# Next keys' products and counts in columns that scores leave empty, turned logits later, GpSimd's subtraction in two

## The chip, the cores and the metric

One core of one Trainium2 chip. The metric is the device time of one execution in microseconds (us), the median of three runs. The engines are named as in the profile: PE is TensorE's matmuls, PEld its weight loads, DVE VectorE, ACT ScalarE, POOL GpSimd, SP the engine whose queue issues most DMAs.

## The reference, cut to what matters

Attention over keys that are averaged from 4 x 4 blocks, and behind it a mixture of experts with one expert for each token. Four batches of 12288 tokens with 128 channels, 768 keys a batch, 8 experts with 1024 hidden units.

```python
kv_pool = kv.reshape(B, H // r, r, W // r, r, C).mean(axis=(2, 4))
k = v = kv_pool.reshape(B, -1, C) @ w_sr
s = q @ k.transpose(0, 2, 1) / np.sqrt(C)
a = np.exp(s - s.max(-1, keepdims=True))
a /= a.sum(-1, keepdims=True) + 1e-09
x = (a @ v).reshape(B * S, D)
logits = x @ w_gate
e_idx = np.argmax(logits, axis=1)
gate_w = softmax(logits)[np.arange(N), e_idx]
eom = 1.0 / (1.0 + np.exp(-(x @ w_output_gate)))
for e in range(E):
    h = np.maximum(x[mask] @ w1[e], 0.0)
    out[mask] = gate_w * eom[:, e] * (h @ w2[e])
```

## The kernel before, in words

The 49152 tokens are worked on in 96 groups of 512 (`NG`; 24 groups a batch, `GPB`). Nearly every product is split in fp16 halves, high and low, and made of three matmuls. For each batch one expert is chosen from the mean key, and all tokens go through it; tokens that want another expert are put on lists in DRAM and done at the end.

The order of work is written out by hand. The main loop runs over iterations `i` (one group enters in each) and eight steps `s`; `now[0]` is `8 * i + s`. In a step, the letters of `ORD` "shxryfue" say in which order things are issued: `s` the scores of 128 tokens (`qk`, on even steps, j = s // 2), `h` a hidden block of the expert for the group two iterations back (`moe_h`: H, HH on ScalarE, HL on VectorE), `x` the exponential (`qk_exp`), `r` the rounding of the probabilities (`qk_round`, on odd steps), `y` the expert's second product (`moe_y`), `f` a stage of the routing at step 5, `u` the product of probabilities and values (`pv`, which makes U and its two halves), `e` what `at(n, f)` has put down for this step. Behind the letters come, at the end of the step, the loads of queries, the next batch's keys (`kp`, the generator `kv_prep`), the transposes of probabilities (`p_turn`, a DMA on SP's queue), the splitting of weights (`w_split`) and the routing (`routes`). Each engine runs its instructions in the order in which they are issued.

PSUM has three pools: `psA` with two buffers of two banks (the scores S and whatever takes a tile "A"), `psH` with three of one bank (H, U, the logits, the turned logits), `psY` with one. A score uses columns 0 to 383 of each bank. Columns 384 to 511 hold the output's transposes (`moe_turn`, L822, for j of 2 and 3) and, through `hooks`, other small products: a hook is a function that is called with the S tile of the first score of j 0 or 1 (`HJ`; any j while i is 7 or less) from a given step on, ahead of its score's matmuls (L475 to L478), one for each S.

A score's way: PE makes S (L483 to L487), VectorE its maximum (L489, L490), ScalarE the exponential `pr` (L504, two buffers) and its fp16 rounding `ph` (L517), GpSimd the low half, `pr - ph`, as one operation of 128 x 768 (L518), SP's queue transposes both halves into PT (L523), and PE multiplies with the values (L540).

The next batch's keys (`kv_prep` with `fast` false, batches 1 to 3): for each of six blocks GpSimd adds rows (L296 to L300), five steps later PE transposes the sums into a psA tile kvt (L304), ScalarE copies them (L307), two steps later PE multiplies with w_sr into another psA tile kvk (L239), ScalarE copies the keys out (L240). Then the largest key is transposed in a psA tile vmp (L330) and read by `largest` (L170, L171), the fp16 halves K2 are made, V2 is transposed by DMA (L372), the expert is chosen through a hook (L376, L250), its weights are loaded (L717 to L722) and split by `w_split` (L770 to L778).

The routing runs once for a unit of four groups: `logits` (L550), `logits_turn` (L576) one step later (`RG`), then the generator `routing` (L594), a stage at a time: L611 to L617, L620 to L626, L628 to L637, then a hook with `counts` (L642, L643) for the next step on, L656 to L661, L663, the wait for the counts, their copy `cnt` out of S (L667), and so on to the list's rows, sixteen indirect DMAs on GpSimd's queue (L705).

Of the kernel before, what the change touches and what calls it, by code (L numbers as in the profile page):

```python
# [20 lines left out]
F32 = mybir.dt.float32  # L21
# [11 lines left out]
P = 128  # L33
# [21 lines left out]
class Cfg:  # L55
# [13 lines left out]
    SK, SO = 30, 15  # L69
    RG = 1  # L70
    RSEQ = (1, 2, 1, 1)
# [9 lines left out]
          (16, 0, (1, 1, 0)), (18, 0, (2, 1, 0), (1, 1, 1)), (20, 0, (2, 1, 1)))  # L81
    PRB = 2
    QL, QT, QN = 0, 3, 6
    QLA = ((7,), (7,)) + ((0, 3, 6),) * 6
# [16 lines left out]
def body(ctx, tc, q, kv, w_sr, w_gate, w_og, w1, w2, out, cfg=Cfg):  # L101
# [66 lines left out]
    def largest(m, ps):  # L168

        dve.tensor_reduce(out=m, in_=ps, op=ALU.max, axis=AX.X)  # L170
        dve.scalar_tensor_tensor(m, m, 2.0 ** -100, m, op0=ALU.max, op1=ALU.max)  # L171

# [58 lines left out]
    def kv_prep(b, fast):  # L231
# [4 lines left out]
        def keys(k, ps, pT):  # L236

            kk = ts(k, P)
            pe.matmul(ps[:, 1, 0:P], wsr, pT, start=True, stop=True)  # L239
            act.activation(kT[:, kk], ps[:, 1, 0:P], AF.Copy, accum_out=vs[:, k:k + 1])  # L240
# [33 lines left out]
        for k in range(NKB):  # L274
# [25 lines left out]
            pool.tensor_tensor(y[:, 1, 0:128], x[:, 1, 0:128], x[:, 1, 128:256], op=ALU.add)  # L300
            for _ in range(5):
                yield
            ps = psA.tile([P, 2, 512], F32, tag="A", name=f"kvt{b}_{k}")
            pe.transpose(ps[:, 0, 0:P], y[:, 1, 0:128], ident)  # L304
            KVN[b][1] += 1
            pT = kvp.tile([P, P], F32, tag="pT", name=f"pT{b}_{k}")
            act.activation(pT, ps[:, 0, 0:P], AF.Copy, scale=1.0 / 16.0)  # L307
            yield
            yield
            keys(k, psA.tile([P, 2, 512], F32, tag="A", name=f"kvk{b}_{k}"), pT)  # L310
            yield
        e2 = kvp.tile([P, 7], F32, tag="ve2", name=f"ve2{b}")
# [13 lines left out]
        if not fast:  # L326
            for _ in range(3):
                yield
        ps = psA.tile([P, 2, 512], F32, tag="A", name=f"vmp{b}")
        pe.transpose(ps[:, 0, 0:P], mxb, ident)  # L330
        if fast:
# [3 lines left out]
            warm(cfg.WM[1])  # L335
        largest(e2[:, 5:6], ps[:, 0, 0:P])
        powers(e2[:, 0:1], e2[:, 1:2], e2[:, 5:6])
# [122 lines left out]

    hooks, now, mid = [], [0], [False]
    spare = {"n": 0}

# [46 lines left out]
    def qk_round(i, j):  # L510

        pr = PR.pop((i, j))
        ph = wk.tile([P, 2, NK], F16, tag="ph", bufs=3, name=f"ph{i}_{j}")
        if j in cfg.PHD and i < LAG:
            dve.tensor_copy(ph[:, 0, :], pr)
        else:
            act.activation(ph[:, 0, :], pr, AF.Copy)  # L517
        pool.tensor_tensor(ph[:, 1, :], pr, ph[:, 0, :], op=ALU.subtract)  # L518
        PH[(i, j)] = (ph, None, now[0])
# [64 lines left out]

    WF = {}
    SCT = set()

# [6 lines left out]
    def routing(c):  # L594
# [11 lines left out]
        def T3(nm, n=E, bufs=1):  # L606
            return T(nm, n, F32, bufs).rearrange("p (b e) -> p b e", e=n)
# [33 lines left out]
        def counts(S):  # L641
            pe.matmul(S[:, 0, 384:384 + E], ones16, oh16, start=True, stop=True)  # L642
            pe.matmul(S[:, 1, 384:384 + E], tri16, oh16, start=True, stop=True)  # L643
            ps.append(S)

        ending = g0 + ng + 2 >= NG
        cnt = rt.tile([P, 2, E], F32, tag="cnt", name=f"cnt{c}")
        if ending:
            for _ in range(cfg.LC[c == NU - 1]):
                yield  # L650
            counts(psA.tile([P, 2, 512], F32, tag="A", name=f"cps{c}"))
            dve.tensor_copy(cnt, ps[0][:, :, 384:384 + E])
        else:
            hooks.append((now[0] + 1, counts))
        se = T("se")
        dve.tensor_reduce(out=se, in_=dn, op=ALU.add, axis=AX.X)  # L656
        zz = T3("dn")
        dve.tensor_tensor(zz, L[:, :, E:2 * E], oh, op=ALU.mult)
# [5 lines left out]
        while not ps:  # L664
            yield
        if not ending:
            dve.tensor_copy(cnt, ps[0][:, :, 384:384 + E])  # L667
        yield
# [13 lines left out]
        yield  # L682
        st = rt.tile([P, E], F32, tag="st", name=f"st{c}")
        dve.scalar_tensor_tensor(st, cnt[:, 1, :], -1.0, ebase, op0=ALU.add, op1=ALU.add)
        x1 = T3("x1")
# [7 lines left out]

        nd = rt.tile([P, E], F32, tag="nd", name=f"nd{c}")
        dve.scalar_tensor_tensor(nd, w8, cho, cnt[:, 0, :], op0=ALU.not_equal, op1=ALU.mult)
        dve.tensor_tensor(ebase, ebase, nd, op=ALU.add)
        rw = T3("rw", RW, 3)
        pool.tensor_copy(rw[:, :, 0:1], scl.unsqueeze(2))
# [287 lines left out]
    with tc.manual_schedule(engines={pool.engine, sp.engine, pe.engine, act.engine, dve.engine}):  # L986
# [32 lines left out]

        events = {}  # L1020

        def at(n, f, *args):
            events.setdefault(8 * i + s + n, []).append((f, *args))

        def after_values(ri, rc):
            if rc is not None:
                logits(rc)

                def turn():
                    logits_turn(rc)  # L1030
                    rts.append([routing(rc), 0, rc])
                at(cfg.RG, turn)
            n = max(0, 8 * cfg.UD + cfg.UDS * ri - now[0])
            at(cfg.UT + n, u_turn, ri)
            at(cfg.UO + n, u_out, ri)
# [190 lines left out]
```

## Time and profile before

| | us |
|---|---|
| median of 3 runs | 1962.98 (1962.57 to 1963.02) |
| the profiled execution | 1944.66 |
| its span, first to last instruction | 1942.9 |
| PE busy | 1870.8 (96%) |
| DVE busy | 1504.7 (77%) |
| ACT busy | 1321.3 (68%) |
| POOL busy | 1159.8 (60%) |

The profile is of one execution. Busy times are sums over the span; a matmul's end is modelled, and matmuls overlap in their pipeline. An idle time in brackets or in a list of waits is the time in which the engine ran nothing, with the instruction that ended it.

### The profile page before, as it was taken

What the parts mean: (1) busy time and instruction counts of PE and PEld (TensorE: products, weight loads), DVE (VectorE), ACT (ScalarE), POOL (GpSimd) and SP (SyncE); (2) the same over time, 40 slices, a digit from 0 to 9 for tenths busy, and PEclk for the clock granted to TensorE, in tenths of its full rate; (3) what the DMA queues carried; (4) which work ended last, traced back from release to release, by engine and by line L of the source; (5) the groups of instructions that cost most, each with busy time, mean ns of one, the idle gap of its engine ahead of it and who ended that gap; (6) DMA issues with size and microseconds to landing.
All of it is one profiled execution on the core that took longest, in us unless ns stands there. A gap on an engine that the chain in (4) does not pass through costs nothing. (4 is left out here: it accounts for less than half of the span.)

```text
span 1942.9 us, 31028 instructions
## 1 busy us (share of the span) xinstructions
PE 1870.8 (96%) x10225; PEld 951.0 (49%) x10225; DVE 1504.7 (77%) x3005; ACT 1321.3 (68%) x2391; POOL 1159.8 (60%) x996
## 2 busy tenths in 40 slices
PE   6999999999999999999999999999999999999997
PEld 4444455454445544545444554444445555545544
DVE  6776877888878778788787787787877877877773
ACT  3767767676776766676767776667677767767653
POOL 2537566564675676754756656656466456466462
PEclk9999999999999999999999999999999999999999
DMA  8877788788988887878788988778778778786642
GB/s 234 161 153 160 168 163 180 153 163 169 183 170 165 170 178 159 168 145 187 141 168 172 187 174 169 162 155 151 167 148 167 152 147 166 154 159 142 133 105 70
DMA packets 884017, 311.63 MB, mean 160 GB/s; under 512 B 827584, under 2 KB 833857, under 8 KB 883856
## 3 DMA queue, kind: packets, MB, share of 16 engines
q1 hardware_dynamic: 870944, 309.18, 78.7%
q0 software_dynamic: 12480, 0.40, 0.5%
q8 instruction: 81, 1.33, 0.3%
q14 instruction: 80, 0.66, 0.1%
q10 hardware_dynamic: 432, 0.07, 0.0%
HBM read 56.83 MB, written 51.25 MB: 56 GB/s over the span
## 5 line engine op out<-in xcount | busy, mean ns | idle before, releaser
L518 POOL TENSOR_TENSOR ph<-pr,ph 128x768 f16<-128x768 f32 x384 | 633.0, 1649 | 629.5 <-ACT ph L517 383.2
L796 DVE SCALAR_TENSOR_TENSOR HL<-H,HH 128x512 f16<-128x512 f32 x768 | 526.0, 686 | 142.3 <-ACT HH L795 127.9
L795 ACT ACTIVATE HH<-H 128x512 f16<-128x512 f32 x768 | 456.5, 594 | 246.6 <-PE H L792 240.3
L504 ACT ACTIVATE pr<-S,nm,qm 128x768 f32<-128x768 f32 x384 | 381.0, 992 | 240.2 <-DVE nm L490 222.7
L705 POOL DMA_INDIRECT scr<-rw,idx x384 | 383.1, 998 | 95.8 <-issue 88.1
L489 DVE TENSOR_REDUCE nm<-S 128x1 f32<-128x768 f32 x384 | 365.3, 951 | 86.8 <-PE S L487 86.3
L540 PE MATMUL U<-PT,V 128*128 128x512 f16 (+1 forms) x1746 | 406.1, 378 | 7.4 <-DVE HL L796 5.1
L517 ACT ACTIVATE ph<-pr 128x768 f16<-128x768 f32 x380 | 319.9, 842 | 2.4 <-DMA PT<-ph 1.9
L790 PE MATMUL H<-U,w 128*128 128x512 f16 x768 | 292.3, 381 | 12.3 <-DVE HL L796 7.0
L791 PE MATMUL H<-U,w 128*128 128x512 f16 x768 | 292.1, 380 | 0.0
L807 PE MATMUL Y<-HL,w 128*128 128x512 f16 x768 | 291.3, 379 | 0.7 <-DVE HL L796 0.6
L792 PE MATMUL H<-U,w 128*128 128x512 f16 x768 | 291.7, 380 | 0.0
L805 PE MATMUL Y<-HH,w 128*128 128x512 f16 x768 | 291.4, 379 | 0.3 <-ACT ys L810 0.3
L806 PE MATMUL Y<-HH,w 128*128 128x512 f16 x768 | 291.3, 379 | 0.0
L540 PEld LDWEIGHTS <-V 128*128 128x128 f16 x1746 | 171.4, 98 | 212.6 <-issue 11.5
L483 PE MATMUL S<-K,qT 128*128 128x384 f16 x768 | 189.2, 328 | 13.1 <-ACT pr L504 7.5
L487 PE MATMUL S<-K,qT 128*128 128x384 f16 x768 | 189.0, 328 | 1.3 <-DVE qT L459 1.0
L485 PE MATMUL S<-K,qT 128*128 128x384 f16 x768 | 188.9, 328 | 0.5 <-DVE K L349 0.5
L825 DVE TENSOR_TENSOR o<-S,msw 128x256 f32<-128x256 f32 x176 | 74.8, 425 | 89.0 <-ACT pr L504 87.6
L792 PEld LDWEIGHTS <-w 128*128 128x128 f16 x768 | 75.3, 98 | 91.4 <-issue 1.4
L807 PEld LDWEIGHTS <-w 128*128 128x128 f16 x768 | 75.2, 98 | 90.8 <-issue 0.3
L805 PEld LDWEIGHTS <-w 128*128 128x128 f16 x768 | 75.2, 98 | 88.3 <-issue 0.5
(209 smaller groups left out, 1865.4 us busy)
## 6 DMA issues: line engine op xcount, KB each, us to landing
kvs<-in_kv_dram SPq DMA_DIRECT2D x96, 256.0 KB
q<-in_q_dram SPq DMA_DIRECT2D x96, 256.0 KB
urows<-uT SPq DMA_DIRECT2D x96, 256.0 KB
out_dram<-o SPq DMA_DIRECT2D x96, 256.0 KB
PT<-ph SPq DMA_TRANSPOSE x384
scr<-rw,idx POOLq DMA_INDIRECT x384
wr<-in_moe_w_dram SPq DMA_DIRECT2D x8, 512.0 KB
tw<-in_moe_w_dram SPq DMA_DIRECT2D x4, 512.0 KB
```

What stands on the lines that cost most here:

```text
L489: dve.tensor_reduce(out=nm[:, 0:1], in_=S[:, :, 0:384], op=ALU.max, axis=AX.XY, negate=True)
L504: act.activation(pr.rearrange("p (a k) -> p a k", a=2), S[:, :, 0:384], AF.Exp, bias=nm[:, 1:2], scale=es, accum_out=SUMS[c][:, bl:bl + 1])
L517: act.activation(ph[:, 0, :], pr, AF.Copy)
L518: pool.tensor_tensor(ph[:, 1, :], pr, ph[:, 0, :], op=ALU.subtract)
L540: pe.matmul(PVP[i][:, cols], ops[n][0], ops[n][1][:, cols], start=(n == 0), stop=(n == len(ops) - 1))
L705: ins = pool.indirect_dma_start(out=scr, out_offset=bass.IndirectOffsetOnAxis(ap=idx[:, bl:bl + 1], axis=0), in_=rw[:, bl, :], in_offset=None,
L790: pe.matmul(H, w1h[:, ts(f, P)], UH, start=True, stop=False)
L792: pe.matmul(H, w1l[:, ts(f, P)], UH, start=False, stop=True)
L795: act.activation(HH, H, AF.Relu)
L796: dve.scalar_tensor_tensor(HL, H, 0.0, HH, op0=ALU.max, op1=ALU.subtract)
L805: pe.matmul(Y, w2h[:, ts(f, P)], HH, start=(f == 0), stop=False)
L807: pe.matmul(Y, w2h[:, ts(f, P)], HL, start=False, stop=(f == NFB - 1))
```

## The change

- In `kv_prep` for batches 1 to 3, the transpose of the sums, the product with w_sr and the transpose of the largest key no longer take psA tiles of their own: they are hooks and use columns 384 to 511 of an S tile. ScalarE's copies of the first two follow in the same step, behind the letters' other work (`at(0, ...)`). The generator waits for each.
- The counts' hook is asked for three steps after the sums and no longer one; the two operations that need the counts (st and nd) read them from S in the same step (`places`), and the copy `cnt` goes. At the end of the program (the last two units) the counts keep a tile of their own.
- The products with the second logits (L658 and what follows) come one stage of the routing later.
- The logits are turned two steps after they are made and no longer one, but for the last groups; on odd steps the routing's first stage is issued with them.
- `largest` takes its lower bound with a one-input operation for each column.
- From the third group on GpSimd's subtraction is made in two halves of 384 columns.

```diff
@@ -67,7 +67,7 @@
-    RG = 1
+    RG = (1, 2)
...
+    PLN = 2
...
     def largest(m, ps):
 
         dve.tensor_reduce(out=m, in_=ps, op=ALU.max, axis=AX.X)
-        dve.scalar_tensor_tensor(m, m, 2.0 ** -100, m, op0=ALU.max, op1=ALU.max)
+        for n in range(m.shape[1]):
+            dve.tensor_scalar(m[:, n:n + 1], m[:, n:n + 1], 2.0 ** -100, None, op0=ALU.max)
...
@@ -298,17 +300,34 @@
-            for _ in range(5):
-                yield
-            ps = psA.tile([P, 2, 512], F32, tag="A", name=f"kvt{b}_{k}")
-            pe.transpose(ps[:, 0, 0:P], y[:, 1, 0:128], ident)
-            KVN[b][1] += 1
+            for _ in range(4):
+                yield
             pT = kvp.tile([P, P], F32, tag="pT", name=f"pT{b}_{k}")
-            act.activation(pT, ps[:, 0, 0:P], AF.Copy, scale=1.0 / 16.0)
-            yield
-            yield
-            keys(k, psA.tile([P, 2, 512], F32, tag="A", name=f"kvk{b}_{k}"), pT)
-            yield
+            done = []
+
+            def sums(S):
+                pe.transpose(S[:, 0, 384:512], y[:, 1, 0:128], ident)
+                at(0, scaled_sums, S)
+
+            def scaled_sums(S):
+                act.activation(pT, S[:, 0, 384:512], AF.Copy, scale=1.0 / 16.0)
+                KVN[b][1] += 1
+                done.append(0)
+
+            def product(S):
+                pe.matmul(S[:, 0, 384:512], wsr, pT, start=True, stop=True)
+                at(0, kept, S)
+
+            def kept(S):
+                act.activation(kT[:, ts(k, P)], S[:, 0, 384:512], AF.Copy, accum_out=vs[:, k:k + 1])
+                done.append(0)
+
+            hooks.append((now[0] + 1, sums))
+            while not done:
+                yield
+            hooks.append((now[0] + 3, product))
+            while len(done) < 2:
+                yield
...
-        ps = psA.tile([P, 2, 512], F32, tag="A", name=f"vmp{b}")
-        pe.transpose(ps[:, 0, 0:P], mxb, ident)
+        if fast:
+            ps = psA.tile([P, 2, 512], F32, tag="A", name=f"vmp{b}")
+            pe.transpose(ps[:, 0, 0:P], mxb, ident)
+            vmp = ps[:, 0, 0:P]
+        else:
+            done = []
+
+            def spread(S):
+                pe.transpose(S[:, 0, 384:512], mxb, ident)
+                done.append(S[:, 0, 384:512])
+
+            hooks.append((now[0] + 1, spread))
+            while not done:
+                yield
+            vmp = done[0]
...
@@ -515,7 +552,8 @@
-        pool.tensor_tensor(ph[:, 1, :], pr, ph[:, 0, :], op=ALU.subtract)
+        for x in [slice(0, NK)] if i < LAG else [ts(h, NK // cfg.PLN) for h in range(cfg.PLN)]:
+            pool.tensor_tensor(ph[:, 1, x], pr[:, x], ph[:, 0, x], op=ALU.subtract)
...
@@ -641,19 +680,29 @@
+        ending = g0 + ng + 2 >= NG
+        st = rt.tile([P, E], F32, tag="st", name=f"st{c}")
+        nd = rt.tile([P, E], F32, tag="nd", name=f"nd{c}")
+
+        def places(S):
+            assert NPL[0] == c
+            dve.scalar_tensor_tensor(st, S[:, 1, 384:384 + E], -1.0, ebase, op0=ALU.add, op1=ALU.add)
+            dve.scalar_tensor_tensor(nd, w8, cho, S[:, 0, 384:384 + E], op0=ALU.not_equal, op1=ALU.mult)
             ps.append(S)
...
-            counts(psA.tile([P, 2, 512], F32, tag="A", name=f"cps{c}"))
-            dve.tensor_copy(cnt, ps[0][:, :, 384:384 + E])
+            S = psA.tile([P, 2, 512], F32, tag="A", name=f"cps{c}")
+            counts(S)
+            places(S)
         else:
-            hooks.append((now[0] + 1, counts))
+            hooks.append((now[0] + 3, lambda S: (counts(S), at(0, places, S))))
         se = T("se")
         dve.tensor_reduce(out=se, in_=dn, op=ALU.add, axis=AX.X)
+        if not ending:
+            yield
         zz = T3("dn")
         dve.tensor_tensor(zz, L[:, :, E:2 * E], oh, op=ALU.mult)
...
-        if not ending:
-            dve.tensor_copy(cnt, ps[0][:, :, 384:384 + E])
...
-        dve.scalar_tensor_tensor(st, cnt[:, 1, :], -1.0, ebase, op0=ALU.add, op1=ALU.add)
...
-        dve.scalar_tensor_tensor(nd, w8, cho, cnt[:, 0, :], op0=ALU.not_equal, op1=ALU.mult)
         dve.tensor_tensor(ebase, ebase, nd, op=ALU.add)
+        NPL[0] = c + 1
...
@@ -1029,7 +1068,10 @@
                 def turn():
                     logits_turn(rc)
                     rts.append([routing(rc), 0, rc])
-                at(cfg.RG, turn)
+                    if now[0] % 2 and att:
+                        rts[-1][1] = 1
+                        next(rts[-1][0])
+                at(cfg.RG[ri < NG - 4], turn)
```

## Rows read from the trace of the kernel before

**Rows 1.** Windows, 60 to 1860: PE, PEld, DVE, ACT, POOL busy, PEclk, DMA.
```profile
60.00:1860.00 1800.00, 1760.89 (x9613) 885.52 (x9611) 1418.80 (x2753) 1262.92 (x2279) 1105.55 (x931) 1.00 0.82 162
```

**Rows 2.** What PE waited for, 60 to 1860: us in total, times, longest.
```profile
PE H L790 <- DVE HL L796: 6.7, 11, 1.3
PE S L822 <- ACT pr L504: 6.6, 5, 2.5
PE U L540 <- DVE HL L796: 5.1, 6, 1.7
PE H L790 <- DVE U L545: 4.7, 11, 1.0
PE S L483 <- ACT pr L504: 4.0, 3, 1.7
PE S L642 <- DVE oh L637: 3.6, 1, 3.6
PE S L483 <- DVE cnt L667: 2.8, 2, 1.7
PE lT L581 <- ACT lgp L563: 1.6, 3, 0.5
```

**Rows 3.** Timeline of PE behind a transpose of sums: start, us, instruction, idle before.
```profile
772.07 0.38 PE L807 MATMUL Y<-HL,w 128*128 128x512 f16 x1
774.96 0.66 PE L822 MATMUL S<-ident,ys 128*128 128x128 f32 x2 [2.51 <-ACT pr L504]
```

**Rows 4.** Windows with a granted clock under full: columns as in rows 1.
```profile
126.50:133.30 6.80, 5.96 (x18) 2.45 (x19) 4.73 (x10) 2.17 (x4) 1.64 (x1) 0.50 0.81 151
775.00:778.40 3.40, 3.40 (x11) 1.77 (x12) 0.82 (x1) 1.91 (x4) 3.08 (x3) 0.51 0.99 213
```

**Rows 5.** Groups of instructions by form: xcount, busy us, mean ns, idle before.
```profile
L518 POOL TENSOR_TENSOR ph<-pr,ph 128x768 f16<-128x768 f32 x384 | 633.0, 1649 | 629.5 <-ACT ph L517 383.2 <-issue 220.4 <-DVE ph L515 21.2
...
L778 POOL TENSOR_TENSOR w<-wr,w 128x512 f16<-128x512 f32 x16 | 18.6, 1164 | 1.1 <-ACT w L774 1.0
...
L658 DVE TENSOR_TENSOR dn<-L,oh 128x128 f32<-128x128 f32 x23 | 35.4, 1537 | 0.8
L684 DVE SCALAR_TENSOR_TENSOR st<-cnt,ebase 128x8 f32<-128x8 f32 x25 | 18.8, 754 | 0.0
...
L658 DVE TENSOR_TENSOR dn<-L,oh 128x96 f32<-128x96 f32 x1 | 0.3, 321 | 0.0
```

**Rows 6.** Timeline, DVE beside POOL: start, us, instruction.
```profile
371.92 1.07 DVE L674 TENSOR_TENSOR sel<-m,ch 128x16 f32<-128x16 f32 x1
...
370.35 2.61 POOL L296 TENSOR_TENSOR kvs<-kvs 128x512 f32<-128x512 f32 x2
372.92 1.63 POOL L518 TENSOR_TENSOR ph<-pr,ph 128x768 f16<-128x768 f32 x1
```

**Rows 7.** What ACT and DVE waited for, whole span: us in total, times, longest.
```profile
ACT pr L504 <- POOL ph L518: 2.0, 4, 0.7
...
DVE o L825 <- ACT pr L504: 87.6, 173, 0.8
```

**Rows 8.** Timeline of batch 1's first Y and weights; source view of L642.
```profile
541.23 0.38 PE L805 MATMUL Y<-HH,w 128*128 128x512 f16 x1
541.44 0.38 PE L806 MATMUL Y<-HH,w 128*128 128x512 f16 x1
...
521.87 1.16 POOL L778 TENSOR_TENSOR w<-wr,w 128x512 f16<-128x512 f32 x1
...
L642 PE MATMUL S<-oh,ones x23: 169/169/189, 127.3 to 1821.9; 128*128 128x8 f16 x23
```

**Rows 9.** Timeline of DVE at the end of an iteration with routing.
```profile
207.83 1.49 DVE L658 TENSOR_TENSOR dn<-L,oh 128x128 f32<-128x128 f32 x1
...
210.41 0.94 DVE L489 TENSOR_REDUCE nm<-S 128x1 f32<-128x768 f32 x1
```

More of the change, by code (lines that the diff above doesn't have):

```diff
@@ L335, in kv_prep @@
             warm(cfg.WM[1])
-        largest(e2[:, 5:6], ps[:, 0, 0:P])
+        largest(e2[:, 5:6], vmp)
         powers(e2[:, 0:1], e2[:, 1:2], e2[:, 5:6])
@@ L461, in body, with at @@
     hooks, now, mid = [], [0], [False]
+    events = {}
+    def at(n, f, *args):
+        events.setdefault(now[0] + n, []).append((f, *args))
     spare = {"n": 0}
@@ L585, in body @@
     WF = {}
+    NPL = [0]
     SCT = set()
@@ L643, in counts @@
             pe.matmul(S[:, 1, 384:384 + E], tri16, oh16, start=True, stop=True)
+        ending = g0 + ng + 2 >= NG
[5 more added lines that the diff above has]
+            dve.scalar_tensor_tensor(nd, w8, cho, S[:, 0, 384:384 + E], op0=ALU.not_equal, op1=ALU.mult)
             ps.append(S)
-        ending = g0 + ng + 2 >= NG
-        cnt = rt.tile([P, 2, E], F32, tag="cnt", name=f"cnt{c}")
         if ending:
@@ L682, in routing @@
         yield
-        st = rt.tile([P, E], F32, tag="st", name=f"st{c}")
-        dve.scalar_tensor_tensor(st, cnt[:, 1, :], -1.0, ebase, op0=ALU.add, op1=ALU.add)
         x1 = T3("x1")
@@ L692, in routing @@
         dve.scalar_tensor_tensor(idx, sel, BIG, ix, op0=ALU.mult, op1=ALU.add)
-        nd = rt.tile([P, E], F32, tag="nd", name=f"nd{c}")
-        dve.scalar_tensor_tensor(nd, w8, cho, cnt[:, 0, :], op0=ALU.not_equal, op1=ALU.mult)
         dve.tensor_tensor(ebase, ebase, nd, op=ALU.add)
+        NPL[0] = c + 1
         rw = T3("rw", RW, 3)
@@ L1018, in k0 @@
             return cfg.KV0[min(i // GPB, 1)]
-        events = {}
-        def at(n, f, *args):
-            events.setdefault(8 * i + s + n, []).append((f, *args))
         def after_values(ri, rc):
```

## The prediction, made before the change was run

> **What bounds the kernel now.** First read the windows: between 60 and 1860 us TensorE is busy for 1760.89 of 1800 us, VectorE for 1418.80, ScalarE for 1262.92, GpSimd for 1105.55 [rows 1]. So TensorE sets the time and the others matter only where they make it wait. It streams a fixed set of matmuls that the change leaves alone, so the most that any change of this kind can give back is the 39.1 us in which it stands idle there, and somewhat more: a matmul's row lasts 0.38 us while its successor starts 0.21 to 0.22 us after it (541.23 and 541.44, [rows 8]), so each wait hides another 0.17 us. Second, read who ended those waits [rows 2]. They fall into three families. **Ring waits:** a score tile S that waits for the exponential of an earlier S (6.6 us in 5 waits and 4.0 in 3), or for the copy of the counts out of S (2.8 in 2), and once a count product that waits for VectorE's one-hot sums (3.6). **Turned logits:** L581 waits for ScalarE's copy (1.6 in 3). **VectorE late:** H and U wait for HL or for U's low half (6.7, 5.1 and 4.7 us in 28 waits). Third, look at one ring wait closely [rows 3]: after the product at 772.07 the transposes into the next S wait 2.51 us for an exponential. S has two buffers. In the code, each transpose and product of the next batch's keys (kvt, kvk, vmp) takes a buffer of the same pool, so the score behind it needs the buffer of the score just before it, not of the one before that. Fourth, the granted clock [rows 4]: it is at 0.50 or 0.51, the 1.2 GHz level, in three stretches between 60 and 1860 us, 6.80, 3.40 and 3.40 us long (the third, at 1239, is like the second, whose row stands); they begin in or just behind the three longest waits, 3.6 us and twice 2.51 us, and elsewhere the clock is full.
>
> **The change, part by part.**
>
> *Keys' products, counts and the largest key in empty columns of S.* 39 tiles (13 for each of three batches) leave the ring, and the transposes and products ride in columns 384 to 511 of S tiles with j of 0 or 1, where the output transposes do not lie. TensorE's work is the same, ScalarE's two copies for a block are the same; they now come just behind the exponential of the same S in ScalarE's queue, which cannot delay that exponential. The counts are read out in the step that makes them and not a routing stage later, and their product is asked for three steps after the sums instead of one, so the 3.6 us wait goes too. Gone: 6.6 + 4.0 + 2.8 + 3.6 = 17.0 us in 11 waits [rows 2], plus 11 x 0.17 = 1.9, so 18.9. With the three longest waits I let the low clock go: in it TensorE was busy 5.96 and twice 3.40 us [rows 4], half of which is lost, 6.4 us. Together 25.3. Bounds: 0 if the waits only change their name, 25.3 if all go. I take it all: with a score every second step and two buffers, an S can meet an exponential this late only where a tile of the keys has turned the ring one place too far, or where the counts still hold a buffer, and the changed code has neither.
>
> *Turned logits.* One or two steps later for all but the end; the first stage of the routing is issued with them on odd steps, which carry no maximum over scores. The copy they wait for is then long done: 1.6 + 3 x 0.17 = 2.1 us. Bounds 0 and 2.1; I take 2.1. The turned tile sits in the H pool for no longer than before.
>
> *GpSimd's subtraction in two.* From 768 to 512 elements a row falls from 1649 to 1164 ns [rows 5], so 1.9 ns an element and some 0.19 us of fixed cost; two halves of 384 cost about 2 x 0.92 = 1.84 us, 0.195 more. Times 376 (all but the eight of the first two iterations) that is 73 us more of GpSimd, which has the room [rows 1]. What of it reaches TensorE is bounded by 0 and 73 us. The exponential waited for a subtraction only 4 times, 2.0 us in all [rows 7], so nearly all hides in the two pr buffers; I take 2 us.
>
> *What VectorE gets for it.* L658 and L684 read two SBUF tensors. L658 takes 1537 ns on average but 321 for 96 columns at the end, where no subtraction runs; by columns that is 428 at most for 128, so 1.1 us of each of 23 is a wait [rows 5]. Who ends it: L674 at 371.92 is over at 372.99, just after the end of the two L296 (372.96) that it ran beside, although the next subtraction had been started at 372.92 [rows 6]. So VectorE is let in between two GpSimd instructions, and halving one halves the longest wait. Freed: about half of L658's wait (23 x 0.55 = 13 us), nearly all of L684's 18.8 us, since st is now made from PSUM and one SBUF tensor. Besides, L658 moves one stage back. Today it stands ahead of the maximum of the last scores: that row starts only at 210.41, behind the L658 of 207.83 [rows 9]. Against that stands a wait that the change adds: the two reads of the counts by VectorE (places) come right behind the exponential of the same S. How such a read behaves is seen on L825, which also reads columns of S that the exponential does not touch: 87.6 us in 173 waits, 0.5 us each [rows 7]; 23 x 0.5 = 12 us of VectorE, with the next HL and the U behind it, for which TensorE waits. The late-VectorE family is 6.7 + 5.1 + 4.7 + 28 x 0.17 = 21.3 us [rows 2]. Bounds: 0 to 21.3 back. VectorE gains about 31 us and gives back 12, and many of these waits stand behind other work than the routing; I take a third, 7 us.
>
> *The longer way of the next batch's keys.* Counting the steps of the code for batch 1: the last block's sums move by one step, its product by six and the largest key by nine, so K2 and V2 are made eight to nine steps later (step 171 against their first use at 192 and 205: hidden). The expert's choice waits for a first step of an iteration anyway and so moves by exactly one iteration; with it the loads of the weights on SP's queue and their splitting. An iteration is (1821.9 - 127.3) / 22 / 4, about 19.3 us [rows 8]. The subtraction for the first half of w2 ran at 521.87; it would then run at about 541.2 and end at 542.3, and TensorE wants it for the matmul of 541.44 [rows 8]. That is a new wait of 0.9, say 1 us, in batch 1 alone; the later batches begin their loads one iteration earlier. Bounds: 0, and a whole iteration if one more slot is missed.
>
> *largest* with a one-input operation: its few calls can only shorten VectorE's queue; inside the 7 us.
>
> **The sum.** 25.3 + 2.1 + 7 - 2 - 1 = 31.4 us. The profiled execution took 1944.66 us (span 1942.9), so it would take 1913.3. The median of the runs is 1962.98, 18.3 us above the profiled execution for reasons that no row tells; I carry these over unchanged: 1962.98 - 31.4 = 1931.6 us.
>
> **Rivals.**
> 1. *VectorE is not let in between the halves.* The Trainium skill, GPSIMD Engine Reference, section 2.1 Instruction dispatch, says that consecutive Pool instructions are no barrier between its cores: one may start the next while others still write. Then the port might never be free between two halves, and a VectorE instruction would wait for both, 0.195 us longer than today. [Rows 6] speak against that, though there the two halves are different operations. As a mechanism of this kernel: the waits of L658 stay, each subtraction holds VectorE 0.195 us longer, and with the 7 us some 2 more are lost: 1941.
> 2. *The ring waits stay in part.* An S that carries a transpose is given back only after ScalarE's copy behind the exponential. If this delays the score two places on, half of the 18.9 us stays, and half of the clock's 6.2: 1931.6 + 12.7 = 1944. For it: ScalarE's queue also holds the relu copies. Against: a score two places on is four steps away, the wait of 2.51 us arose at half that distance.
> 3. *Slower: each subtraction's extra time is handed on.* Place: the exponential at L504, which needs the pr buffer of two scores before. If GpSimd is behind, as it may be while sixteen list writes stand in its queue, the 0.195 us goes through the exponential to TensorE's next S. All 376 make 73 us; from 43% of them on (31.4 of 73) the kernel is slower than now. With two thirds it is 1931.6 + 49 - 2 = 1979. Against: only 2.0 us of such waits today [rows 7].
> 4. *The weights of batch 1 miss one more iteration.* TensorE then waits some 19 us and comes back at the low clock; priced by the 6.80 us stretch at half rate [rows 4], 3 us more: 1931.6 + 19 + 3 - 1 = 1953.
> 5. *The waits only move* to the next late VectorE row, since it is VectorE that made the exponentials late: 1963.
>
> **How the numbers follow.** The forecast has 0.58, rival 1 0.13, rival 2 0.11, rival 3 0.06, rival 4 0.06, rival 5 0.06. Below the forecast stands the rest of the late-VectorE family: 14.3 us more would be 1917.3. So the range is 1916 to 1950: it takes in rivals 1 and 2 and leaves out 3 to 5, which hold 0.18. A difference under 0.2%, 3.9 us, can't be told from none. Faster: the forecast and rivals 1, 2 and 4, 0.88; same: rival 5, 0.06; slower: rival 3, 0.06.
>
> **What would show it.** In the trace after: no S that waits for an exponential right behind a transpose or product of the keys; no count product waiting near 127 us; the clock full from 60 to 1860 us; subtraction rows of 128x384 near 0.92 us, twice as many less eight; L658 under 1 us; L581 without waits. The sum is wrong if the list of waits shows as much idle time as now with new names, above all scores that wait for an exponential that waited for GpSimd, or a gap at the first Y of batch 1 near 540 us.

## The result, and the profile after

The kernel after takes 1933.0 us (median of 4 runs, 1931.9 to 1936.2) where the kernel before takes 1962.8: a ratio of 0.9851, 95% interval 0.9834 to 0.9868. In two later groups of runs, each on one chip, the ratio was 0.9878 (0.9857 to 0.9899) and 0.9869 (0.9853 to 0.9886). The forecast was 1931.6. The sum of 31.4 us behind it is another matter: the gain was 25 to 30 us, but its terms are not those of the sum.

The list of what PE waited for, 60 to 1860 us of the kernel after (us in total, times, longest), answers to [rows 2]; the window row under it to [rows 1].

```profile
PE H L834 <- DVE HL L840: 10.6, 15, 1.8
PE U L578 <- DVE HL L840: 5.3, 7, 1.8
PE Y L850 <- POOL w L822: 2.3, 1, 2.3
PE H L834 <- DVE U L583: 2.2, 3, 1.0
PE Y L849 <- ACT ys L854: 1.5, 5, 0.4
PE S L866 <- DVE nd L691: 0.9, 1, 0.9
...
60.00:1860.00 1800.00, 1774.60 (x9732) 896.48 (x9732) 1404.36 (x2799) 1269.57 (x2299) 1175.31 (x1324) 1.00 0.83 164
```

The scores that waited for an exponential or for the copy of the counts, and the wait of the count product at 127 us, are gone. One output transpose now waits 0.9 us for the reading of the counts out of its S (nd, L691), another 0.4 us for the copy of key sums that rides in its S. Most of what is left is VectorE's: H and U waiting for HL or U's low half (now L840 and L583) had 16.5 us in 28 waits and have 18.1 in 25.

The forms of the kernel after (count, busy us, mean ns, idle before) answer to [rows 5], the two rows behind them to [rows 7].

```profile
L556 POOL TENSOR_TENSOR ph<-pr,ph 128x384 f16<-128x384 f32 x752 | 674.0, 919 | 521.7 <-issue 423.0 <-ACT ph L554 93.7 <-POOL kvs L298 1.5
...
L707 DVE TENSOR_TENSOR dn<-L,oh 128x128 f32<-128x128 f32 x23 | 9.8, 428 | 0.0
...
L655 DVE SCALAR_TENSOR_TENSOR sume<-SUM,ve 128x16 f32<-128x16 f32 x23 | 13.4, 581 | 0.0
...
L710 DVE TENSOR_TENSOR z<-z,rinv 128x16 f32<-128x16 f32 x23 | 15.3, 666 | 0.8
...
DVE st L690 <- ACT pr L541: 13.8, 23, 0.6
ACT pr L541 <- POOL ph L556: 13.4, 11, 1.5
```

L556 is the subtraction (L518 before), L707 the product with the second logits (L658), L710 and L655 its neighbours in the routing (L661 and L616 before).

**The main stretch.** The source view of the exponential gives the start of the first and of the last one; the line for before, then after:

```profile
L504 ACT ACTIVATE pr<-S,nm,qm x384: 979/991/1066, 33.7 to 1854.2; 128x768 f32<-128x768 f32 x192
```

```profile
L541 ACT ACTIVATE pr<-S,nm,qm x384: 980/991/1016, 33.4 to 1828.1; 128x768 f32<-128x768 f32 x192
```

The main stretch is 26.1 us shorter, but the profiled executions differ by 12.7 only (1944.66 and 1931.92). The rest is lost behind the last exponential: before ends 88.7 us after it, after 102.1. The kernel after has a stretch of 10.4 us there in which PE stands still and ACT and DVE nearly do (1.8 and 2.5 us busy). The clock falls to 0.50 within it, for 10.2 us, and PE works in the last 4.3 of them; the profiled execution of before had neither. The third group of experiments tells whose that is.

### The profile page after: what moved, and what is told of

Same layout as the page of the kernel before. It is cut to its first block, busy times and chain, and to the rows that moved or that the text cites. A ratio compares the mean times of both kernels' runs of the same rounds, so it can differ in the third digit from the quotient of the medians.

```text
span 1930.2 us, 31486 instructions
## 1 busy us (share of the span) xinstructions
PE 1861.7 (96%) x10225; PEld 950.6 (49%) x10225; DVE 1472.0 (76%) x2984; ACT 1318.7 (68%) x2391; POOL 1217.4 (63%) x1372
## 5 line engine op out<-in xcount | busy, mean ns | idle before, releaser
L556 POOL TENSOR_TENSOR ph<-pr,ph 128x384 f16<-128x384 f32 (+1 forms) x760 | 687.1, 927 | 547.3 <-issue 423.0
L840 DVE SCALAR_TENSOR_TENSOR HL<-H,HH 128x512 f16<-128x512 f32 x768 | 526.4, 686 | 173.9 <-ACT HH L839 146.6
L749 POOL DMA_INDIRECT scr<-rw,idx x384 | 387.6, 1009 | 94.9 <-issue 91.0
L578 PEld LDWEIGHTS <-V 128*128 128x128 f16 x1746 | 170.7, 98 | 212.2 <-issue 11.2
```

The source lines that it names most:

```text
L556: pool.tensor_tensor(ph[:, 1, x], pr[:, x], ph[:, 0, x], op=ALU.subtract)
L578: pe.matmul(PVP[i][:, cols], ops[n][0], ops[n][1][:, cols], start=(n == 0), stop=(n == len(ops) - 1))
L749: ins = pool.indirect_dma_start(out=scr, out_offset=bass.IndirectOffsetOnAxis(ap=idx[:, bl:bl + 1], axis=0), in_=rw[:, bl, :], in_offset=None,
L840: dve.scalar_tensor_tensor(HL, H, 0.0, HH, op0=ALU.max, op1=ALU.subtract)
```

## The experiments

The change has three separable parts: **keys** (products of the next keys in columns of S), **routing** (counts and places, turned logits, the added stage) and **halves**. The question is which of them carries the gain. All ratios are to the kernel before, run beside it on the same chip; the start of the last exponential is used to compare main stretches across chips. It is good to some 3 us: two traces of before have 1854.2 and 1852.4, three of after 1828.1, 1831.1 and 1828.4. Line numbers differ from kernel to kernel, the names of the tiles do not.

### Single parts, and all but the halves

Keys alone is the hunk of `kv_prep`, routing alone the hunks of `routing`, `after_values` and `RG`, both with the new place of `at`. The hunk of `largest` is in neither, only in the kernel after and what is made from it by a constant; it was not run alone (its operations take 8.8 us of VectorE in all before, 1.6 after). Halves alone, in the kernel before:

```diff
-        pool.tensor_tensor(ph[:, 1, :], pr, ph[:, 0, :], op=ALU.subtract)
+        for x in [slice(0, NK)] if i < LAG else [ts(h, NK // cfg.PLN) for h in range(cfg.PLN)]:
+            pool.tensor_tensor(ph[:, 1, x], pr[:, x], ph[:, 0, x], op=ALU.subtract)
```

Everything but the halves, in the kernel after:

```diff
-    PLN = 2
+    PLN = 1
```

> The kernel before with the keys' part of the change alone: sums, product and largest key ride in empty columns of S. Theory (the ring turns one place too far at each key tile): the S waits for an exponential go (6.6 and 4.0 us), those for the counts' copy with them (2.8), and the two 3.4 us stretches at half clock; with 0.17 us hidden at each wait some 18 us less than before by the time of the last exponential (before: 1854.2 us), and the weights of batch 1 late by about 1 to 2 us. Rival (S tiles that carry a transpose come free too late): half of that, about 9 us, with S waits left in the list. Second rival (the waits only move): within 4 us of before.

> The kernel before with the routing's part alone: counts read in the step that makes them, asked for three steps later, second logits one stage later, logits turned two steps later. Theory: the wait of 3.6 us at 127 us goes with its 6.8 us at half clock (3 us), L581 stops waiting (2.1), and of the waits for a late VectorE a third: about 12 to 15 us less than before by the last exponential; the key tiles' ring waits stay. Rival (VectorE waits for the exponential ahead of the two reads of the counts, 23 times 0.5 us): the waits for HL and U grow instead and only the 8.8 us of the first two terms come.

> The kernel before with GpSimd's subtraction in two halves alone. Theory (VectorE is let in between the halves): L658 falls from 1537 ns to about 1000, L684 by a third; of the waits for HL and U 2 to 5 us go, about 2 us are lost to the longer subtraction: 0 to 4 us less than before. Rival (VectorE waits for both halves): L658 grows to about 1.7 us, 2 to 4 us more than before. Rival (the longer subtraction is handed on through pr): up to 73 us more.

> The kernel after with the subtraction whole again. Theory: the halves are worth 2 to 5 us on VectorE's side there too, so 0 to 4 us more than after. Rival (the halves cost more on GpSimd than they give VectorE): 2 to 4 us less than after. In the profiled execution after there is a wait of 10.4 us near 1870 us in which TensorE, ScalarE and VectorE all stand; if it hangs on GpSimd's longer queue, it goes here.

| kernel | time, us | ratio, 95% interval | last exponential, us |
|---|---|---|---|
| before, same chip | 1941.52 | | 1854.2 (first trace) |
| keys | 1934.17 | 0.9962 (0.9949 to 0.9974) | 1844.7 |
| routing | 1955.87 | 1.0072 (1.0053 to 1.0091) | 1867.1 |
| halves | 1933.37 | 0.9958 (0.9937 to 0.9978) | 1843.0 |
| keys and routing (all but the halves) | 1940.69 | 0.9992 (0.9983 to 1.0002) | 1851.0 |

*Keys* takes every wait of a score for an exponential or for the counts' copy away, 13.4 us, and gives most of it back. Its PE waits, 60 to 1860 us:

```profile
PE H L825 <- DVE HL L831: 10.7, 16, 1.8
PE H L825 <- DVE U L580: 6.7, 12, 1.0
PE U L575 <- DVE HL L831: 5.0, 6, 1.7
PE S L677 <- DVE oh L672: 3.8, 1, 3.8
PE lT L616 <- ACT lgp L598: 3.2, 6, 0.8
PE Y L841 <- POOL w L813: 2.5, 1, 2.5
```

H and U now wait 22.4 us for VectorE, 5.9 more than in [rows 2], the turned logits 1.6 more, and the first Y of batch 1 waits 2.5 for its weights; the count product's wait (3.8) is routing's to remove. *Routing* alone is slower, where a gain of 12 to 15 us was expected of it. Its forms on DVE and its PE waits:

```profile
L622 DVE SCALAR_TENSOR_TENSOR sume<-SUM,ve 128x16 f32<-128x16 f32 x23 | 27.8, 1210 | 0.0
L677 DVE TENSOR_TENSOR z<-z,rinv 128x16 f32<-128x16 f32 x23 | 26.4, 1150 | 0.8
L698 DVE TENSOR_TENSOR x<-x,st 128x128 f32<-128x128 f32 x23 | 21.6, 941 | 0.0
...
PE Y L818 <- DVE HL L807: 8.7, 13, 1.5
PE H L801 <- DVE HL L807: 8.3, 14, 1.2
PE U L545 <- DVE HL L807: 7.9, 10, 2.5
```

In the kernel before the same three operations took 347, 259 and 533 ns. The product with the second logits did leave the subtraction's way (from 1537 ns to 408), which is 26 us of VectorE; but the three operations that came into its way cost 23 x (863 + 891 + 408 ns) = 50 us. Two scores also wait 4.7 us for the new reading of the counts (nd). And *all but the halves* is the kernel before again: 0.9992. The ring waits are gone there too, and its H, U and Y wait 33.5 us for VectorE:

```profile
PE H L834 <- DVE HL L840: 16.4, 19, 1.8
PE U L578 <- DVE HL L840: 8.1, 10, 2.5
PE Y L851 <- DVE HL L840: 5.9, 9, 1.5
PE H L834 <- DVE U L583: 3.1, 4, 1.0
```

So without the halves, the two parts on which some 26 of the 31.4 us were put bring nothing together, and the halves, taken at 2 us of cost against 7 of gain, are what separates 0.9992 from 0.987. Halves alone had 0 to 4 us expected; it brought 8. The product with the second logits, still in its old stage, falls from 1537 ns to 796:

```profile
L660 DVE TENSOR_TENSOR dn<-L,oh 128x128 f32<-128x128 f32 x23 | 18.3, 796 | 0.8
```

### Pairs with the halves, and the weights' split earlier

Three kernels and the kernel after again, on another chip. Pairs are put together from the hunks above; the earlier split is

```diff
-    WTN = 10
+    WTN = 8
```

> The kernel after, again, beside the kernel before and beside single parts on one chip. Measured so far against before on one chip: keys alone 0.9962, halves alone 0.9958, routing (counts, places, turn, added stage) alone 1.0072, keys and routing with the whole subtraction 0.9992. If the parts add up, the whole is 0.9992 - 0.0042 = 0.995 of before (1932 us where before is 1941.5). If the two halves are what lets the routing's move pay (its late VectorE work no longer waits for a whole subtraction), it is below that, 0.985 to 0.992. The wait of 10 us near 1870 us, in which TensorE, ScalarE and VectorE stand together while GpSimd writes lists: if it belongs to the program, it is in this trace again; if it is an accident of one execution, the last exponential is again near 1828 us and the end about 88 us behind it, not 102.

> Before with two of the three parts: the keys' products in columns that scores leave empty, and the subtraction in two operations; routing's counts, places, turn of logits and its added stage stay as before. If the parts add up: 1941.5 - 7.4 - 8.2 = 1925.9 where before is 1941.5 (ratio 0.992), and this is 6 us or more below the kernel after, so that the routing's part is a loss in after too. If routing's part pays once the subtraction is halved, this is above the kernel after by 2 us or more, with the wait of the count product near 127 us (2.8 to 3.8 us and 6.8 us at half clock) in it.

> Before with routing's part and the halved subtraction, without the keys' part. If the parts add up: 1941.5 + 14.4 - 8.2 = 1947.7 where before is 1941.5 (ratio 1.003). If routing's loss alone was that its late VectorE work stood behind whole subtractions, halving takes most of the loss away: 1930 to 1936 (0.994 to 0.997), z*rinv and the sums of exponentials under 1 us each where routing alone had over 22 us of excess on each of the two, and the ring waits of scores for exponentials behind keys still there (about 13 us).

> After, with the second matrix of the gated part split two steps earlier in each batch (one constant, 10 to 8). The trace of after has 2.3 us of TensorE waiting for GpSimd's part of that split at the first Y of batch 1, and 3.4 us at half clock right behind it. Theory that this is the weights' being late: both are gone, last exponential 3 to 4 us earlier, time 3 to 4 us below that of after on this chip. Rival, that the wait only hands on what GpSimd is behind by: the split comes two steps earlier but so does its load on GpSimd, subtractions are later by the same, and the time is within 1 us of that of after.

| kernel | time, us | ratio, 95% interval | last exponential, us |
|---|---|---|---|
| before, same chip | 1959.40 | | not traced |
| after, again | 1934.03 | 0.9878 (0.9857 to 0.9899) | 1831.1 |
| keys and halves | 1940.59 | 0.9898 (0.9877 to 0.9920) | 1836.4 |
| routing and halves | 1948.55 | 0.9948 (0.9931 to 0.9964) | 1845.8 |
| after, weights' split earlier | 1934.71 | 0.9876 (0.9859 to 0.9892) | 1832.1 |

By the last exponential, routing makes the main stretch 12.9 us longer alone, 2.8 longer with halves (1843.0 to 1845.8), 6.3 longer with keys (1844.7 to 1851.0) and 5 to 8 us shorter with both (1836.4 to 1831.1 on the same chip, 1828.1 on another; here `largest` comes in too). Halving is worth 11.2 us alone, 8.3 with keys, 21.3 with routing and some 20 to 23 with both. The parts don't add up: routing puts two-input operations of VectorE where GpSimd's subtraction starts, and how long they stand there is set by the length of a piece. The two that took 1210 and 1150 ns in routing alone take 733 and 632 in routing and halves. Why routing then gains beside keys and halves is shown only in part: 6.9 us of waits of turned logits go, H and U wait 18.7 us where they waited 12.3, and PE's two lists come to nearly the same total (25.7 and 25.4 us).

The timeline shows that at one place of the routing, DVE beside POOL (start, us, instruction). All but the halves first, with the product of PE that waits, then after (its trace of the third group):

```profile
1290.39 1.63 POOL L556 TENSOR_TENSOR ph<-pr,ph 128x768 f16<-128x768 f32 x1 [1.59 <-ACT ph L554]
1290.45 1.61 DVE L710 TENSOR_TENSOR z<-z,rinv 128x16 f32<-128x16 f32 x1
1291.98 0.68 DVE L840 SCALAR_TENSOR_TENSOR HL<-H,HH 128x512 f16<-128x512 f32 x1
1292.71 0.38 PE L851 MATMUL Y<-HL,w 128*128 128x512 f16 x1 [1.15 <-DVE HL L840]
```

```profile
1272.71 1.78 POOL L556 TENSOR_TENSOR ph<-pr,ph 128x384 f16<-128x384 f32 x2 [1.46 <-ACT ph L554]
1272.77 0.88 DVE L710 TENSOR_TENSOR z<-z,rinv 128x16 f32<-128x16 f32 x1
1273.58 0.68 DVE L840 SCALAR_TENSOR_TENSOR HL<-H,HH 128x512 f16<-128x512 f32 x1
```

A product of 16 columns, 0.17 us where nothing is in its way, ends with the subtraction that began 0.06 us before it; with two pieces it ends with the first piece, and the HL behind it is done 0.72 us sooner after the subtraction's start. PE waits 1.15 us for that HL with the whole subtraction and not at all with two pieces. The Trainium skill (SBUF — State Buffer, SBUF: two separate sides) says that a VectorE instruction with two inputs in SBUF and a GpSimd instruction that reads SBUF exclude each other: whichever starts first has the shared ports for the whole instruction. These rows agree, with GpSimd first (1.61 and 0.88 us).

*The weights' split earlier* takes the new wait at the first Y of batch 1 away. In the kernel after that wait is this:

```profile
532.12 1.15 POOL L822 TENSOR_TENSOR w<-wr,w 128x512 f16<-128x512 f32 x1
533.33 0.44 PE L850 MATMUL Y<-HH,w 128*128 128x512 f16 x1 [2.27 <-POOL w L822]
...
533.50:536.90 3.40, 3.40 (x9) 1.22 (x8) 1.28 (x3) 1.29 (x4) 3.37 (x4) 0.50 0.71 187
```

2.27 us, and behind it a window at 0.50, the 1.2 GHz level. With the earlier split no Y waits for w, and nothing is won: 1934.71 beside 1934.03. H and U wait 22.6 us for VectorE where they wait 18.7 in the kernel after on that chip. The rival held: the wait was handed on. That the subtractions come later by as much, as the rival has it, is not shown.

Nor does the low clock belong to this wait. In the trace of after on that same chip the Y waits 2.27 us as well, and the window right behind it is at full clock:

```profile
534.30:537.70 3.40, 3.40 (x20) 1.84 (x19) 1.95 (x4) 2.69 (x6) 3.37 (x4) 1.00 0.67 185
```

Its half clock, 6.8 us, begins at 986.6, behind a wait for HL of 1.81 us and in one for U of 0.98; with the earlier split 3.4 us stand at 941.8 behind one of 1.80. The second trace of before likewise has the 3.6 us wait of the count product and full clock behind it (6.50 us at 1.00 from 127.5). So which wait costs clock changes from one execution to the next.

### Whose the 18 us are, and a third piece

Before had taken 1962.8 us beside the first runs of after, 1941.5 beside the single parts and 1959.4 beside the pairs. Before and after, each with a trace on one chip, and after with

```diff
-    PLN = 2
+    PLN = 3
```

> The kernel before, with its trace, on the chip of this call. Its time has been 1962.8 where the kernel after took 1933.0, 1959.4 where after took 1934.0, and 1941.5 beside the single parts, whose traces have no wait of all engines behind the main stretch. Theory: those 18 us are that wait (10 us in which TensorE, ScalarE and VectorE stand while GpSimd writes lists, and 10 us at half clock behind it), which belongs to the chip and not to the program. Then the trace has it exactly if the time is near 1960: last exponential near 1854 us either way, the end about 105 us behind it with the wait and 88 us behind it without. Rival, that the main stretch itself is longer on those chips: the last exponential is near 1872 us, the end 88 us behind it.

> The kernel after on the chip of this call. Main stretch as before on other chips, last exponential at 1828 to 1832 us. If the wait behind the main stretch belongs to the chip: end 102 us behind the last exponential and 1933 us where before takes 1960, but 88 us behind it and 1916 to 1920 us where before takes 1941. If the wait belongs to this program: 1933 us on every chip, so 0.4% from before where before takes 1941.

> After with the subtraction of probabilities in three operations of 256 columns (one constant, 2 to 3). With one operation the last exponential of this kernel was at 1851.0 us, with two at 1828.1 and 1831.1. Theory that VectorE's being let in between GpSimd's operations is what the halves bring: its waits shorten again by a third to a half of what the first cut brought, HL and U family on TensorE from 19 to about 13 us, last exponential 4 to 8 us earlier, 1925 to 1930 us where after takes 1933. Rival that two operations bring it all and a third only adds GpSimd's fixed time (0.19 us by 376 = 73 us more of its span): within 2 us of after, or up to 5 us slower.

| kernel | time, us | ratio, 95% interval | last exponential, us | from it to the end, us |
|---|---|---|---|---|
| before | 1943.26 | 1.0001 (0.9991 to 1.0010) | 1852.4 | 88.7 |
| after | 1917.83 | 0.9869 (0.9853 to 0.9886) | 1828.4 | 88.0 |
| after, three pieces | 1902.53 | 0.9793 (0.9777 to 0.9810) | 1812.3 | 88.1 |

The same kernel after takes 1917.8 us here and 1934.0 on the chip of the pairs, 16.2 more. 13.4 of these lie behind the last exponential (88.0 against 101.4 us), 2.7 in the main stretch. Windows of the stretch in question (us, PE, PEld, DVE, ACT, POOL, PEclk), first where after takes 1934, then where it takes 1918:

```profile
1861.00:1871.00 10.00, 8.86 (x40) 3.70 (x38) 5.90 (x22) 2.14 (x4) 7.67 (x8) 1.00 0.16 53
1871.00:1881.00 10.00, 1.37 (x7) 1.01 (x7) 2.47 (x15) 1.68 (x3) 6.84 (x11) 0.65 0.02 0
1881.00:1891.00 10.00, 10.00 (x40) 4.23 (x39) 6.64 (x25) 4.18 (x7) 0.00 (x0) 0.84 0.10 28
```

```profile
1858.00:1868.00 10.00, 9.96 (x49) 4.63 (x48) 8.74 (x39) 5.06 (x9) 7.56 (x9) 1.00 0.16 53
1868.00:1878.00 10.00, 9.96 (x48) 4.55 (x47) 6.90 (x24) 4.49 (x8) 6.22 (x10) 1.00 0.11 29
1878.00:1888.00 10.00, 9.96 (x47) 4.36 (x45) 5.61 (x9) 4.82 (x9) 4.45 (x6) 1.00 0.85 250
```

GpSimd goes on with its list writes in both. In the first, ScalarE runs three instructions in ten microseconds, and VectorE and PE stand behind it; two rows of its list of waits, 1864 to 1882 us:

```profile
ACT HH L839 <- remote: 8.7, 2, 5.0
PE ot L881 <- ACT HH L839: 8.6, 1, 8.6
```

So the wait belongs to the chip or the moment and not to the change: it is in all five traces of changed kernels taken beside a before of 1959 to 1963 us, whatever the kernel, and in none of the eight taken beside one of 1941 to 1943. For the kernel after this is shown; chip and moment can't be told apart, since each group had one chip. That before's 18 us are the same wait is inferred: the two traces of before have none, and their executions took 1944.66 and 1942.76. What ScalarE waited for is open; its row says only "remote", no event of this core.

The third piece was expected to bring 4 to 8 us and brought 15.3, or 16.1 by the last exponential. H, U and Y wait 9.7 us for VectorE, against 18.2 with two on the same chip:

```profile
PE H L834 <- DVE HL L840: 4.4, 9, 1.0
PE U L578 <- DVE HL L840: 3.8, 6, 1.8
PE H L834 <- DVE U L583: 1.0, 2, 0.6
PE Y L851 <- DVE HL L840: 0.5, 2, 0.3
```

PE's whole list is 10.3 us shorter up to the last exponential, 12 waits fewer hide some 2.0, and no half clock is left where 3.4 us were (1.7); some 2 us have no row. One rare case is in the difference. The sums of the probabilities once took 3.36 us in the kernel after on that chip, and 0.23 with three pieces:

```profile
1411.93 3.36 DVE L655 SCALAR_TENSOR_TENSOR sume<-SUM,ve 128x16 f32<-128x16 f32 x1
1412.36 1.79 POOL L556 TENSOR_TENSOR ph<-pr,ph 128x384 f16<-128x384 f32 x2
1414.10 1.15 POOL L822 TENSOR_TENSOR w<-wr,w 128x512 f16<-128x512 f32 x1
```

Here VectorE was not let in between two pieces, nor ahead of the weights' split; it ended with the third operation. Of 104 instructions of VectorE in that trace that took over 0.15 us more than the shortest of their form behind GpSimd's elementwise operations, 89 ended with the first such operation, 13 with a second, 2 with a third, by a count over the rows. In 30 of the 89 no further operation followed directly, so of the 74 that met a second one without a gap VectorE was let in ahead of it 59 times and passed over 15 times. With three pieces 94 of 100 ended with the first and 3 with a second or third: 64 let in of 67.

### Four pieces

```diff
-    PLN = 2
+    PLN = 4
```

> After with the subtraction in four operations of 192 columns (one constant, 2 to 4). Last exponential with one, two and three operations: 1851.0, 1828.4, 1812.3 us, so the second cut brought 22.6 us and the third 16.1. Theory that each cut shortens what VectorE stands behind: the next piece is 1.643 less three fixed 0.19 us over four, about 0.55 us against 0.68 and 0.92, and the TensorE waits on the HL and U family, 17.6 us with two and 9.2 with three, fall to 4 to 7; last exponential 1805 to 1810 us, ratio to before 0.974 to 0.978 (three: 0.9793). Rival that GpSimd's fixed time now catches up (73 us more of its span, handed on through the probabilities' buffers): last exponential at 1812 us or later, ratio 0.979 to 0.984, with scores waiting for exponentials again.

1908.13 us, ratio 0.9820 (0.9804 to 0.9837); last exponential at 1818.5. Better than two pieces, 5 to 6 us behind three, which ran on another chip. The number lies in the rival's range, but its mechanism is not there: the fixed time is as expected (558 ns a piece), yet the exponential waits for GpSimd only once, 0.2 us, so it is not handed on through `pr`. VectorE's waits are longer again: by the same count 24 of 140 now end with a second or third operation (75 let in of the 99 that met one), and the split of the queries rises to 1002 ns a time from 835 with three:

```profile
L470 DVE SCALAR_TENSOR_TENSOR q<-q,qm,q 128x512 f16<-128x512 f32 x93 | 93.2, 1002 | 0.0
```

Summed up, what these VectorE instructions took over the shortest of their form is 100 us with one piece (all but the halves), 71 with two, 44 with three and 63 with four: the order of the times. Why VectorE is passed over more often with four pieces stays open. Three pieces is the best version seen: 2.1% below the kernel before and 0.8% below the kernel after on the same chip (1902.53 of 1917.83).

## Why the prediction came out

The time came out, and in part by luck. The ring waits were taken at 25.3 us and bring nothing without the halves; the halves were taken at 5 us and bring some 23 on top of the rest. The two errors nearly cancel in the sum. How the 18.3 us were carried over flatters it further (below).

**Ring waits, 25.3 us: gone as said, the gain not kept by this step alone.** Every wait that the step names is gone from the trace, and of the three half-clock stretches between 60 and 1860 us (13.6 us) one of 3.4 us is left, behind the new wait at 533: 4.7 of the 6.4 us. That the clock falls with the longest waits holds for the trace that was read, not in general: in the second trace of before it stays full behind the 3.6 us wait. But the step bounds itself by "0 if the waits only change their name, 25.3 if all go" and takes the upper end, arguing from S's two buffers only. What it lacked is VectorE: keys alone gave back 5.9 us as waits for HL and U, 1.6 as turned logits and 2.5 at the first Y of batch 1, and kept 7.4; keys with routing kept nothing (0.9992). That is rival 5, which held for these two parts alone.

**Halves and VectorE, 7 - 2 us: the size failed twice.** Taking the halving out of the kernel after costs 1.2% (0.9869 to 0.9992), some 23 us, where the step had 5. It bounded the gain by the late-VectorE waits that stand in the trace of before, 21.3 us; but halving also cuts the waits that the other two parts make, which no row of before shows. Measured against before, those waits did not shrink by a third: 16.5 became 18.1 us. The 7 us of gain did not come, and 1.6 were lost: this alone is more than the shortfall, 31.4 forecast against 24 to 26 measured, by the last exponential and by the times where no engine stands at the end (1942.4 to 1917.8, 24.6). The 0.195 us of fixed time is right (1649 to 919 ns a half), its 2 us on the path can't be seen by themselves: the exponential waits for the subtraction 13.4 us where it waited 2.0 [rows 7], and no score in PE's list waits for an exponential behind it.

**L658.** It left the subtraction's way as said: 428 ns, the very figure taken for it. That its neighbours would enter was not seen: L710 from 259 to 666 ns and L655 from 347 to 581, 23 x (407 + 234) = 15 us against the 26 saved (22 in the trace of the third group; with the subtraction whole they take 1215 and 1190 ns, 41 us). L684, the making of st, falls from 754 ns to 167, as said. The price of `places` was right: 12 us forecast, 13.8 measured.

**Turned logits, 2.1:** 0.5 us in one wait is left of 1.6 in 3; as said but for half a microsecond. **Weights of batch 1, 1 us:** the place is right, the wait 2.27 and not 0.9. The experiment shows that taking it away gains nothing.

**Rival 1** is refuted in the main: where a second operation followed directly, VectorE came in ahead of it 59 times of 74, as [rows 6] had it. What it names does happen, in the other 15. The Trainium skill's warning from which it was drawn (GPSIMD Engine Reference, 2.1 Instruction dispatch) says nothing of how often; these counts do. **Rival 2** shows once, 0.4 us, an S that waits for the copy of key sums (its 6.2 us of clock is a slip for 6.4). **Rival 4** did not occur. **Rival 3** has its first half (13.4 us of waits of the exponential), but they do not reach TensorE.

**The 18.3 us carried over** from the profiled execution to the median were real on such a chip, and after pays some 15 to 16 there. Had the median been taken on one of the other chips, the same sum would have given 1911 us against 1917.8 measured. Between the first runs and the third group before differs by 20.4 us and after by 15.2, so some 5 us of the 29.8 measured first are not the change's: that the forecast is only 1.4 us off is luck to this extent.

Up to the last exponential the list of waits fell by 14.5 us (38.2 to 23.7) and the stretch by 26.1. 4.7 of the rest are the half clock, and 16 waits fewer (50 to 34, at 0.17 us each) hide some 2.7; about 4.2 us have no row.

## What to carry to other kernels

Where two engines shut each other out for whole instructions, the length of one instruction on the engine with time to spare is a cost of its own: cut it first, and judge moves of small operations on the other engine with it cut, because a move only changes which operation is caught. Price the parts of a change also as pairs: waits removed at one place come back at the engine that is late next, and its waits in the trace of before are no upper bound for them. Try a constant on both sides of its best value; here one, two, three and four pieces gave 0.9992, 0.987, 0.979 and 0.982 of the time before.

## What the runs showed of the hardware

- The same program ran 16 us longer on one chip than on another: near the end ScalarE (for 5.0 to 7.9 us in one piece, over five traces of such chips), and the engines behind it, stand for some 10 us while GpSimd writes lists, and within this time the clock falls to half for 10.2 us (13.7 in one). The cause is open.
- A subtraction on GpSimd, float16 from float32 into float16, took 1647, 918, 682 and 558 ns for 768, 384, 256 and 192 columns: 1.9 ns a column and 0.19 us fixed.
- VectorE is usually let in between two GpSimd operations that follow each other without a gap, but not always: 59 of 74 times with two pieces, 64 of 67 with three, 75 of 99 with four.
- A wait of TensorE does not always cost clock: behind the same 2.27 us wait at the same instruction the granted clock was 0.50 for 3.4 us in one execution and 1.00 in another.
